# Attention into two chained multilayer blocks: when late weights are loaded and when sums of y are formed

## The chip, the cores and the metric

The kernel runs on one core of a Trainium2 chip. A core has a matrix engine (PE in the rows below, with its weight loads as PEld), a vector engine (DVE), an activation engine (ACT), a general engine (POOL) and a queue that issues transfers (SP). The engines run side by side. Each works through its own instructions in a fixed order and stops where an instruction needs something that another engine has not finished. The metric is the time of one execution in microseconds (us).

## The reference, cut to what matters

```python
# q, k, v: (B=2, H=8, S=768, D=64); blocked local attention and block summaries
x = attention(q, k, v)                # laid out as 1536 tokens x 512
h = maximum(maximum(x @ w1, x @ w2), x @ w3)        # layer one, 512 -> 768
y = h @ w_out                                       # layer two, 768 -> 512
z = ((y @ w_a) * (y @ w_b)) @ moe2_w_out            # layer three 512 -> 1536, layer four 1536 -> 512
```

All is 32-bit float. The kernel splits each operand into a high and a low part, and computes a product as three matmuls (`mm3`), so that every matmul of 128x128 weights by 384 tokens appears three times.

## The kernel before, in words

Tokens are cut into four chunks c = 0 to 3 of 384 tokens; chunks 0 and 1 come from the first batch b = 0, chunks 2 and 3 from the second.

**Layers one and two.** Chunks 0 and 1 go through `layers12` while the attention of the second batch still runs; `TURNS` says how many steps of one stand beside how many of the other. Chunks 2 and 3 go together through `pair1`, a generator of 62 steps: 8 plain steps, then 42 steps that form products with a Strassen-like scheme (seven products for a block of two by two, on sums of weights and of x), then 4 plain steps, then 8 of layer two. The products need sums of weights. `w_sums` makes them: POOL L614 restores a weight, DVE L471 to L474 add and subtract (in `sums4`), ACT L464 and POOL L465 split the sums into the two parts. PE writes the products to banks named hb, hg, hd, the plain products to ph, and layer two to py. Each product leaves its bank through `result`, on DVE L633 (add), L635 (running maximum) and L640 (maximum from the bank), or on ACT.

**Sums of y.** Layer three uses the same scheme on y, so it needs six sums and differences of y's quarters. `sums_of` makes one set a call: `diff` is DVE L749 (a subtraction), `op` is ACT L744 (the high part) and DVE L745 (the low part). For the first batch it works on tiles of 128x768 ("wide" below), in four calls at the steps of `pair1` listed in `SUMS`. For the second batch it works on tiles of 128x384, as layer two delivers y.

**Weights.** A weight tile takes three stages: `w_load` (SP L434, a transfer), `w_round` (ACT L454 and L456, DVE L458 and L459, POOL L460) and `w_split` (ACT L464, DVE or POOL L465, and, for layer three, DVE L471 to L474). `weights(most)` advances up to `most` tiles if `fits` finds room, and runs the first stages of later tiles ahead of the last stage. The tiles from number `N12` = 24 on belong to layers three and four. The first three of them copy one column of a finished hidden tile, the `gate`, into the tile they load to (POOL L433), which holds the transfer back until `gate` exists; `GATE` names the tile.

**Layers three and four.** `layers34` runs over `order34`: a0, b0, a1, o0, b1, a2, o1 and so on, six groups of each kind. Groups a and b are layer three (banks qb, qg, qd; DVE L803 adds a kept product and writes it as ca, DVE L809 and POOL L810 multiply, DVE L537 splits), group o is layer four (PE L842 to L844, DVE L856). The code issues the products of a0 for the first batch before those of the second.

**What sets the order.** The order of SP is the order in which the code asks. For PE, DVE, ACT and POOL a scheduler sorts the instructions when the program is built, from the order of the code, so that an edit in one place can move rows in others. `behind_marks` keeps what is issued inside it behind the latest `result` instructions of its engine. All PSUM banks named h, p and q come from one ring of 8.

Of the kernel before, what the change touches and what calls it, by code (L numbers as in the profile page):

```python
# [42 lines left out]
N1, N2, NK = 3 * FF1 // P, FF1 // P, FF2 // P // 3  # L43
N12, N34 = N1 + N2, 9 * NK
# [8 lines left out]

W64, W32, WBUFS, QB, FB, SM, GB, BANKS = (6, 3), (4, 3), (24, 10), 4, (9, 1), 2, (12, 9), (2, 2, 1, 2, 2)

GATE, ROOM, SUMS, EARLY34 = (2, 1), 16, (40, 43, 46, 49), 6
PLAIN, XSUMS, WSUMS, WS, PT, MAX_G, LO_G, ASK = (2, 1), (2, 4), (5, 7), 8, 7, False, True, (0, 2)
RING, LEAD, TURN, ERA0, ASKS, AHEAD, PRE, TURNS = 8, 5, (11, 2, 4), 10, (3, 4, 5, 7, 9), (4, 1), 3, ((6, N1 - 6, 6, 4, 4), (24, 34), (34, 43))

# [10 lines left out]
def attention_then_maxout_then_bilinear(ctx: ExitStack, tc: tile.TileContext, qt, kt, vt, vwin, wall, const, out):  # L78
# [57 lines left out]
    @contextmanager  # L136
    def behind_all(*names):

        with ExitStack() as pins:
            for name in names:  # L140
                if name in marks:
                    pins.enter_context(tc.issue_after(marks[name]))
            yield
# [274 lines left out]
    order34 = [("a", 0)] + [x for n in range(NG) for x in (("b", n), ("a", n + 1), ("o", n)) if x[1] < NG]  # L418
# [9 lines left out]
    def w_load(q):  # L428
        first = q < N12
        w64_t[q] = w64_p.tile([P, 512], U64, tag="w64e" if q < ERA0 else f"w64{first}", name="w64",  # L430
                              bufs=ERA0 if q < ERA0 else W64[not first])
        if q in range(N12, N12 + W64[1]):
            G.tensor_copy(w64_t[q].bitcast(F32)[:, 0:1], gate[0])  # L433
        nc.sync.dma_start(out=w64_t[q], in_=wall[seq[q]])  # L434

    def w_ask(n):

        while w_at[0] < n:
            w_load(w_at[0])
            w_at[0] += 1  # L440
# [51 lines left out]
    w_at, w_done, w_freed, w_room = [0, 0, 0], 0, 0, 0  # L492

    def fits(n):

        return n <= N12 or n - w_freed <= ROOM and n - max(N12, w_freed) <= WBUFS[1]

    def weights(most):

        nonlocal w_done, w_room  # L500
        for _ in range(most):
            if w_done == len(seq) or not fits(w_room + room[w_done]) or w_done == N12 and not gate:
                return
            w_room += room[w_done]
            w_done += 1
            ahead = min(AHEAD[0] + 2 * (w_done < ERA0 + 4), W64[w_done + AHEAD[0] > N12] - 2 * (w_done >= ERA0 + 4))
            for n, (step, more) in enumerate(((w_load, ahead), (w_round, AHEAD[1]), (w_split, 0))):
                while w_at[n] < min(w_done + more, len(seq) if gate else N12):
                    step(w_at[n])
                    w_at[n] += 1  # L510
# [4 lines left out]
    def flush():  # L515
        while late:
            late.pop(0)()
# [251 lines left out]
    def layer3(kind, n, cs):  # L769

        nonlocal w_freed
        ws = w_t[kind, n]
        ps, kept = {}, {}
        each = [(i, b) for i in range(7) for b in range(B)]
        if (kind, n) in (order34[0], order34[-2]):
            each.sort(key=lambda x: x[1])
        for i, b in each:
            w, y, bank_ = PRODUCTS[i]
            first = (b, bank_) not in ps
            if first:  # L780
                ps[b, bank_] = ps_m.tile([P, 512], F32, tag="r", name=f"q{bank_}", bufs=RING)[:, 0:MAXT * P]
            (wt, o), to = ws[w], ps[b, bank_]
            with behind_all("po"):
                for k in range(2):
                    ins = mm3(to, wt, o + k * P, ops[b, y][:, :, k], first and k == 0, k == 1, not first)
            if (kind, n) == order34[-2]:
                marks["po"] = ins
            flush()

            def evac(i=i, b=b, to=to):  # L790
                def keep(name):
                    kept[b, name] = t = half(name)
                    A.activation(t, to, AF.Copy)

                def result(f, j, x):

                    c = 2 * b + j
                    if kind == "a":
                        cs[c, f] = t = half("ca")
                        if x is None:  # L800
                            A.activation(t, to, AF.Copy)
                        else:
                            V.tensor_tensor(t, to, x, ALU.add)  # L803
                        return
                    t = half("t")
                    if x is None:
                        V.tensor_tensor(t, to, cs[c, f], ALU.mult)
                    else:
                        V.tensor_tensor(t, to, x, ALU.add)  # L809
                        G.tensor_tensor(t, t, cs[c, f], ALU.mult)  # L810
                    gs[n, c, f] = g = hg_p.tile([P, 2, MAXT * P], F32R, tag="g", name="hg", bufs=GB[1])
                    split(g, t, V)

                if i in (0, 1, 2):
                    keep(("s1", "m5", "u2")[i])
                elif i == 3:
                    result(0, 0, kept[b, "s1"])
                elif i == 4:
                    result(1, 1, kept[b, "m5"])
                elif i == 5:  # L820
                    result(0, 1, kept[b, "u2"])
                else:
                    result(1, 0, None)

            late.append(evac)
            yield
        w_freed += 3
# [3 lines left out]
    def layer4(n, q):  # L831
        nonlocal w_freed
        for c in (1, 0, 3, 2) if n == NG - 1 else range(NCH):
            for i in range(CHUNKS[c][2]):
                parts = 2 if (n, c, i) == (NG - 1, 2, MAXT - 1) else 1
                for j in range(parts):
                    cols_ = slice(j * DM // parts, (j + 1) * DM // parts)
                    ps = ps_m.tile([P, 512], F32, tag="r", name="po", bufs=RING)[:, cols_]
                    with behind_all("po"):
                        for f in range(2):  # L840
                            w, g = w_t[q + f][:, :, cols_], gs[n, c, f][:, :, i * P:(i + 1) * P]
                            T.matmul(ps, g[:, 0], w[:, 0], start=(f == 0), stop=False)  # L842
                            T.matmul(ps, g[:, 0], w[:, 1], start=False, stop=False)  # L843
                            ins = T.matmul(ps, g[:, 1], w[:, 0], start=False, stop=(f == 1)).ins  # L844
                    if n == NG - 1:
                        marks["po"] = ins
                    flush()

                    def evac(c=c, i=i, ps=ps, cols_=cols_):
                        if n == 0:  # L850
                            if not acc:
                                sums = acc_p.tile([P, NCH, MAXT, DM], F32, tag="acc", name="acc", bufs=1)
                                acc.update({(c, i): sums[:, c, i] for c in range(NCH) for i in range(MAXT)})
                            V.tensor_copy(acc[c, i], ps)
                        else:
                            V.tensor_tensor(acc[c, i][:, cols_], ps, acc[c, i][:, cols_], ALU.add)  # L856
                        if n == NG - 1:
                            r0 = (CHUNKS[c][0] * NT + CHUNKS[c][1] + i) * P
                            nc.sync.dma_start(out=out[r0:r0 + P, cols_], in_=acc[c, i][:, cols_])

                    late.append(evac)
                yield
        w_freed += 2

    def layers34():
        q, cas = N12, {}
        for kind, n in order34:
            if kind == "o":
                flush()
                yield from layer4(n, q)  # L870
            else:
                yield from layer3(kind, n, cas.setdefault(n, {}))
            q += 2


# [15 lines left out]
    for i, c in enumerate(turns):  # L891
        next(dense[int(c)])

        n = i + 1 if i < TURNS[0][0] else TURNS[0][0] + (i - TURNS[0][0]) // 2 + 1 if i < 2 * N1 - TURNS[0][2] else i + TURNS[0][2] - N1 + 1
# [10 lines left out]
    next(dense[-1], None)  # L905
    for i, _ in enumerate(pair1()):
        with behind_marks():
            weights(1)
            if i in SUMS:
                m = SUMS.index(i)  # L910
                sums_of(m // 2, m % 2 * 2 + 1)
    for _ in layers34():
        weights(2)
    flush()


# [54 lines left out]
```

## Time and profile before

| | us |
|---|---|
| median of 3 runs | 550.06 |
| lowest and highest | 549.61 and 550.55 |
| profiled execution, its own time | 549.45 |
| its span in the profile | 547.2 |

A span is the time from the first to the last instruction that the profiler saw; what lies between it and the execution's own time (2.2 us here) is start and end. A row of a timeline gives the start, the busy time, the engine, the line of the kernel, the operation, what it writes and reads, and in brackets how long the engine had been idle before and what ended that. Times in a timeline are counted from the start of the span.

### The profile page before, as it was taken

To read this page: it belongs to the slowest core of one execution; us is meant where nothing else is said; L and a number is where in the kernel's file an instruction comes from. 1 tells how busy PE (TensorE), PEld (TensorE's weight loads), DVE (VectorE), ACT (ScalarE), POOL (GpSimd) and SP (SyncE) were. 2 spreads that over 40 slices of the span, in tenths; PEclk is the share of its full clock that TensorE was granted. 3 is DMA by queue.
4 is the path that set the end of the run, shared out by engine and by line. 5 is a ranking of instruction groups with operands and counts; after the bars stand their busy time and mean duration, and the time that the engine had idled before them with its cause. 6 is when DMAs were issued, how large, how long until landed. Compare 5 with 4: busy or idle time off the path is not lost.

```text
span 547.2 us, 9042 instructions
## 1 busy us (share of the span) xinstructions
PE 534.0 (98%) x3328; PEld 506.3 (93%) x3328; DVE 422.2 (77%) x863; ACT 284.6 (52%) x692; POOL 245.9 (45%) x207
## 2 busy tenths in 40 slices
PE   7899999999999999999989999999999999999997
PEld 7789999999999999989989989989998998998986
DVE  5798985885439677699999997985997798574464
ACT  4699775676533342567667645633544543340130
POOL 3479997642239577544334342521621442230120
PEclk9999999999999999999999999999999999999999
DMA  8998334375100000232311241132122121000014
GB/s 297 356 278 294 123 116 151 110 223 165 38 1 1 2 0 1 106 97 107 116 48 68 78 153 40 40 115 78 38 78 78 40 77 40 1 0 1 0 49 183
DMA packets 17132, 51.82 MB, mean 95 GB/s; under 512 B 2112, under 2 KB 2752, under 8 KB 17088
## 3 DMA queue, kind: packets, MB, share of 16 engines
q1 hardware_dynamic: 17088, 51.25, 28.0%
q8 instruction: 26, 0.43, 0.3%
q14 instruction: 18, 0.15, 0.1%
HBM read 48.09 MB, written 3.15 MB: 94 GB/s over the span
## 4 chain that ended last, share of the span: by engine, by line
PE 80%; DVE 9%; POOL 4%; issue 2%; ACT 1%; DMA 1%; DVEq 0%; POOLq 0%; ACTq 0%
PE ph L532 17%; PE qb L532 16%; PE py L532 9%; PE qg L532 8%; PE po L843 6%; PE po L844 6%; PE po L842 6%; PE qd L532 4%; PE ps L261 3%; PE psv L318 2%; PE pst L299 2%; POOL wt L465 1%; DVE yt L745 1%; DVE yd L749 1%; DVE w L459 1%
## 5 line engine op out<-in xcount | busy, mean ns | idle before, releaser
L460 POOL TENSOR_TENSOR w<-w,w 128x512 int32<-128x512 int32 x60 | 85.3, 1431 | 140.5 <-DVE w L459 79.9
L532 PE MATMUL qb<-yt,wt 128*128 128x384 f32 x576 | 109.9, 336 | 1.7 <-DVE ca L803 1.3
L532 PE MATMUL ph<-x,wt 128*128 128x384 f32 x576 | 107.2, 338 | 0.0
L532 PEld LDWEIGHTS qb<-yt,wt 128*128 128x128 f32 x576 | 101.0, 188 | 3.5 <-DVE ca L803 1.6
L532 PEld LDWEIGHTS ph<-x,wt 128*128 128x128 f32 x576 | 99.1, 188 | 0.3
L810 POOL TENSOR_TENSOR t<-t,ca 128x384 f32<-128x384 f32 x36 | 43.7, 1226 | 67.5 <-DVE t L809 67.3
L532 PE MATMUL qg<-yt,wt 128*128 128x384 f32 x288 | 57.8, 335 | 0.5 <-DVE yt L745 0.5
L856 DVE TENSOR_TENSOR acc<-po,acc 128x512 f32<-128x512 f32 (+1 forms) x61 | 40.7, 678 | 22.3 <-PE po L844 22.2
L843 PE MATMUL po<-wt,hg 128*128 128x512 f32 (+1 forms) x146 | 56.6, 387 | 0.0
L844 PE MATMUL po<-wt,hg 128*128 128x512 f32 (+1 forms) x146 | 56.5, 387 | 0.0
L842 PE MATMUL po<-wt,hg 128*128 128x512 f32 (+1 forms) x146 | 56.5, 387 | 0.0
L532 PE MATMUL py<-hg,wt 128*128 128x384 f32 x288 | 54.0, 340 | 1.1 <-DVE pt L640 1.1
L532 PEld LDWEIGHTS qg<-yt,wt 128*128 128x128 f32 x288 | 50.6, 188 | 0.8 <-DVE yt L745 0.8
L532 PEld LDWEIGHTS py<-hg,wt 128*128 128x128 f32 x288 | 49.5, 188 | 1.6 <-DVE pt L640 1.4
L536 ACT ACTIVATE hg<-t 128x384 fp32r<-128x384 f32 x60 | 30.8, 521 | 34.7 <-POOL t L810 28.7
L268 ACT ACTIVATE s<-s,nm 128x120 f32<-128x120 f32 x96 | 36.9, 387 | 20.5 <-DVE nm L267 20.4
L456 ACT ACTIVATE w<-w 128x512 int32<-128x512 uint32 x60 | 39.4, 671 | 4.7 <-DMA w<-wall 4.7
L454 ACT ACTIVATE w<-w 128x512 f32<-128x512 f32 x30 | 20.3, 675 | 41.2 <-DMA w<-wall 41.1
L464 ACT ACTIVATE wt<-w 128x512 fp32r<-128x512 f32 (+1 forms) x60 | 34.7, 583 | 12.9 <-POOL w L460 11.9
L286 POOL TENSOR_TENSOR s<-s,r 128x720 f32<-128x720 f32 x16 | 22.2, 1390 | 42.6 <-DVE r L284 36.0
L465 DVE TENSOR_TENSOR wt<-w,wt 128x512 fp32r<-128x512 f32 (+1 forms) x44 | 33.7, 768 | 1.5 <-ACT wt L464 1.3
L537 DVE TENSOR_TENSOR hg<-t,hg 128x384 fp32r<-128x384 f32 x48 | 34.2, 722 | 0.9 <-ACT hg L536 0.8
(115 smaller groups left out, 990.1 us busy)
## 6 DMA issues: line engine op xcount, KB each, us to landing
w<-wall SPq DMA_DIRECT2D x60, 512.0 KB, 3.4
qv<-qt SPq DMA_DIRECT2D x15, 384.0 KB, 6.1
row<-kt SPq DMA_DIRECT2D x8, 416.0 KB, 3.6
full<-vt SPq DMA_DIRECT2D x8, 384.0 KB, 6.2
out<-acc SPq DMA_DIRECT2D x11, 256.0 KB, 2.0
qv<-vwin SPq DMA_DIRECT2D x12, 192.0 KB, 5.3
qv<-vwin SPq DMA_DIRECT2D x12, 96.0 KB, 5.0
qv<-qt SPq DMA_DIRECT2D x1, 256.0 KB, 4.5
```

Source lines behind the costliest of these rows:

```text
L268: A.activation(s[:, a], s[:, a], AF.Exp, bias=nm[:, a:a + 1], scale=-1.0, accum_out=sm[:, a:a + 1])
L456: A.activation(lw.bitcast(I32), lw, AF.Copy, scale=2.0 ** -29)
L460: G.tensor_tensor(w.bitcast(I32), w.bitcast(I32), lw.bitcast(I32), ALU.add)
L464: A.activation(w[:, 0], r, AF.Copy)
L465: eng.tensor_tensor(w[:, 1], r, w[:, 0], ALU.subtract)
L532: ins = T.matmul(ps, w[:, i, o:o + P], x[:, j], start=first and n == 0, stop=last and n == 2, skip_group_check=more).ins
L537: ins = eng.tensor_tensor(dst[:, 1], src, dst[:, 0], ALU.subtract).ins
L810: G.tensor_tensor(t, t, cs[c, f], ALU.mult)
L842: T.matmul(ps, g[:, 0], w[:, 0], start=(f == 0), stop=False)
L843: T.matmul(ps, g[:, 0], w[:, 1], start=False, stop=False)
L844: ins = T.matmul(ps, g[:, 1], w[:, 0], start=False, stop=(f == 1)).ins
L856: V.tensor_tensor(acc[c, i][:, cols_], ps, acc[c, i][:, cols_], ALU.add)
```

## The change

The first loads of layers three and four are asked for at step 38 of `pair1` (two at once), and from step 43 on one tile is advanced at every second step until four are done; before, `weights(1)` was called at every step and `fits` and `gate` decided. In `layers34` a tile is advanced only if it belongs to the groups needed soon; before, up to two were advanced at every step that had room. The four calls of `sums_of` in `pair1` come at steps 32, 37, 42 and 47 and not at 40, 43, 46 and 49. The gate is a later hidden tile, the early weights have 9 tiles of their own for loads and not 10, the hidden tiles of layer three 8 and not 9, and the last stretch of attention shares its time with one more step of layers one and two.

```diff
-... GB, BANKS = ..., (12, 9), (2, 2, 1, 2, 2)
+... GB, BANKS = ..., (12, 8), (2, 2, 1, 2, 2)
-GATE, ROOM, SUMS, EARLY34 = (2, 1), 16, (40, 43, 46, 49), 6
+GATE, ROOM, SUMS, EARLY34, ASK34 = (2, 3), 16, (32, 37, 42, 47), 6, (38, 43, 4)
-... ERA0, ASKS, ... TURNS = ... 10, ... ((6, N1 - 6, 6, 4, 4), (24, 34), (34, 43))
+... ERA0, ASKS, ... TURNS = ... 9, ... ((6, N1 - 6, 6, 4, 4), (24, 34), (34, 44))

-        for kind, n in order34:
+        for j, (kind, n) in enumerate(order34):
             if kind == "o":
                 flush()
-                yield from layer4(n, q)
-            else:
-                yield from layer3(kind, n, cas.setdefault(n, {}))
+            for _ in layer4(n, q) if kind == "o" else layer3(kind, n, cas.setdefault(n, {})):
+                yield j
             q += 2

     for i, _ in enumerate(pair1()):
         with behind_marks():
-            weights(1)
+            if i == ASK34[0]:
+                w_ask(N12 + W64[1] - 1)
+            if i >= ASK34[1] and (i - ASK34[1]) % 2 == 0 and w_done < N12 + ASK34[2]:
+                weights(1)
             if i in SUMS:
                 m = SUMS.index(i)
                 sums_of(m // 2, m % 2 * 2 + 1)
-    for _ in layers34():
-        weights(2)
+    for g in layers34():
+        if w_done < N12 + 2 * (g + 2) + 2 * (order34[g][0] == "o"):
+            weights(1)
     flush()
```

What the built program makes of it is seen in the order of DVE. The first place is the last call of `w_sums`, whose sums (L471 to L474, written to s) are the weights of the last group of products; yt and y are the sums of y. A line with + stands only in the changed kernel, a line with - only in the one before.

```order
 L471 TENSOR_TENSOR s<-rc 128x256
 L635 TENSOR_TENSOR pt<-pt 128x384
+L745 TENSOR_TENSOR yt<-y,yt 128x768
 L633 TENSOR_TENSOR pt<-hg,u_2731 128x384
 L635 TENSOR_TENSOR pt<-pt 128x384
 L472 TENSOR_TENSOR s<-s,rc 128x256
 L473 TENSOR_TENSOR s<-rc 128x256
+L640 TENSOR_TENSOR pt<-hb,pt 128x384
 L635 TENSOR_TENSOR pt<-pt 128x384
 L474 TENSOR_TENSOR s<-rc,s 128x256
```

One wide row of the sums of y moved ahead of L472. The second place is the stretch that ends with the last maximum on a bank hb, the first L640 below; layer two's second product reuses that bank. Before, its last twelve rows read:

```order
L635 TENSOR_TENSOR pt_2966<-pt_2966,pt_2958 128x384
L749 TENSOR_TENSOR yd_2969<-y_2131,y_1927 128x768
L635 TENSOR_TENSOR pt_2988<-pt_2988,pt_2980 128x384
L465 TENSOR_TENSOR wt_2837<-w32_2826,wt_2837 128x512
L749 TENSOR_TENSOR yd_3003<-y_2131 128x768
L471 TENSOR_TENSOR s_2859<-w32_2833 128x256
L459 SCALAR_TENSOR_TENSOR w32_2855<-psw_2852,w32_2855 128x512
L473 TENSOR_TENSOR s_2860<-w32_2826,w32_2833 128x256
L745 TENSOR_TENSOR yt_2971<-y_2131,yt_2971 128x768
L465 TENSOR_TENSOR wt_2871<-w32_2833,wt_2871 128x256
L749 TENSOR_TENSOR yd_2999<-y_2131,yd_2969 128x768
L640 TENSOR_TENSOR pt_3026<-hb_2840,pt_2997 128x384
```

In the changed kernel they read as follows, with two wide L749 right ahead of them and L459 of the third weight moved behind L640:

```order
L745 TENSOR_TENSOR yt_2882<-y_2121,yt_2882 128x768
L633 TENSOR_TENSOR pt_3002<-hg_2846,u_2878 128x384
L458 TENSOR_SCALAR w32_2934<-psw_2931 128x512
L635 TENSOR_TENSOR pt_2959<-pt_2959,pt_2926 128x384
L465 TENSOR_TENSOR wt_2908<-w32_2897,wt_2908 128x512
L471 TENSOR_TENSOR s_2938<-w32_2904 128x256
L473 TENSOR_TENSOR s_2939<-w32_2897,w32_2904 128x256
L465 TENSOR_TENSOR wt_2950<-w32_2904,wt_2950 128x256
L745 TENSOR_TENSOR yt_2882<-yd_2982,yt_2882 128x768
L635 TENSOR_TENSOR pt_3002<-pt_3002,pt_2968 128x384
L745 TENSOR_TENSOR yt_2882<-yd_2986,yt_2882 128x768
L640 TENSOR_TENSOR pt_3026<-hb_2820,pt_3011 128x384
```

From L633 of the last hb product (a little ahead of these rows) up to this L640, the kernel before has three L749, one L745 and one L459 where the changed one has two L749 and three L745. The third place is the stretch ahead of the second L803, which must have read the bank qb before the last product of a0's first batch goes on in it. Before:

```order
L465 TENSOR_TENSOR wt_3499<-w32_3190,wt_3499 128x512
L458 TENSOR_SCALAR w32_3495<-w64_3491 128x512
L745 TENSOR_TENSOR yt_3348<-yd_3369,yt_3348 128x384
L458 TENSOR_SCALAR w32_3506<-w64_3502 128x512
L459 SCALAR_TENSOR_TENSOR w32_3495<-w64_3491,w32_3495 128x512
L459 SCALAR_TENSOR_TENSOR w32_3506<-w64_3502,w32_3506 128x512
L803 TENSOR_TENSOR ca_3413<-qb_3351,m5_3388 128x384
```

And in the changed kernel:

```order
L745 TENSOR_TENSOR yt_3294<-yd_3317,yt_3294 128x384
L745 TENSOR_TENSOR yt_3302<-yd_3323,yt_3302 128x384
L465 TENSOR_TENSOR wt_3656<-w32_3632,wt_3656 128x512
L458 TENSOR_SCALAR w32_3772<-w64_3768 128x512
L459 SCALAR_TENSOR_TENSOR w32_3772<-w64_3768,w32_3772 128x512
L803 TENSOR_TENSOR ca_3367<-qb_3305,m5_3342 128x384
```

Between that L640 and this L803 the changed kernel has the same kinds of rows, but three wide L745 fewer and one L459 more. From the second group of layers three and four on, the order of DVE and PE is the same in both (the last 269 rows of DVE and the last 1207 of PE).

## Rows read from the trace of the kernel before

**Rows 1.** The page: span, and busy time of each engine.

```profile
span 547.2 us, 9042 instructions
PE 534.0 (98%) x3328; PEld 506.3 (93%) x3328; DVE 422.2 (77%) x863; ACT 284.6 (52%) x692; POOL 245.9 (45%) x207
```

**Rows 2.** Busy time by stretch: us, then PE, PEld, DVE, ACT, POOL; clock; DMA.

```profile
127.00:187.00 60.00, 60.00 (x493) 57.82 (x493) 35.62 (x105) 28.39 (x96) 27.68 (x22) 1.00 0.09 29
...
204.00:223.30 19.30, 18.60 (x104) 17.54 (x102) 14.09 (x22) 7.42 (x16) 14.49 (x13) 1.00 0.00 1
...
243.40:267.30 23.90, 23.35 (x134) 23.35 (x135) 23.90 (x39) 16.75 (x32) 9.92 (x6) 1.00 0.24 89
...
285.20:520.00 234.80, 234.79 (x1240) 220.32 (x1241) 187.98 (x314) 105.42 (x213) 76.48 (x61) 1.00 0.16 54
```

**Rows 3.** Waits from 204 to 290 us: total, times, longest.

```profile
PE qb L532 <- DVE ca L803: 1.3, 1, 1.3
...
PE py L532 <- DVE pt L640: 1.1, 1, 1.1
...
PE qg L532 <- DVE yt L745: 0.5, 1, 0.5
...
PE hg L532 <- ACT wt L464: 0.4, 1, 0.4
```

**Rows 4.** Timeline of PE, 221 to 288 us.

```profile
221.73 0.44 PE L532 MATMUL hg<-xs,wt 128*128 128x384 f32 x1 [0.40 <-ACT wt L464]
...
236.65 4.15 PE L532 MATMUL ph<-x,wt 128*128 128x384 f32 x23
240.64 2.25 PE L532 MATMUL py<-hg,wt 128*128 128x384 f32 x12
243.95 23.17 PE L532 MATMUL py<-hg,wt 128*128 128x384 f32 x132 [1.06 <-DVE pt L640]
...
272.64 0.44 PE L532 MATMUL qg<-yt,wt 128*128 128x384 f32 x1 [0.49 <-DVE yt L745]
...
282.70 1.21 PE L532 MATMUL qb<-yt,wt 128*128 128x384 f32 x6
285.21 2.38 PE L532 MATMUL qb<-yt,wt 128*128 128x384 f32 x12 [1.31 <-DVE ca L803]
```

**Rows 5.** Timeline of DVE, 219 to 285 us.

```profile
219.78 1.23 DVE L472 TENSOR_TENSOR s<-s,rc 128x256 f32<-128x256 f32 x1
...
225.81 1.52 DVE L745 TENSOR_TENSOR yt<-y,yt 128x768 fp32r<-128x768 f32 x1 [1.93 <-ACT yt L744]
...
227.71 0.94 DVE L745 TENSOR_TENSOR yt<-y,yt 128x768 fp32r<-128x768 f32 x1
228.58 0.54 DVE L633 TENSOR_TENSOR pt<-hb,m 128x384 f32<-128x384 f32 x1
...
233.45 1.28 DVE L459 SCALAR_TENSOR_TENSOR w<-psw,w 128x512 uint32<-128x512 uint32 x2
234.65 0.55 DVE L633 TENSOR_TENSOR pt<-hb,m 128x384 f32<-128x384 f32 x1
...
243.35 0.55 DVE L640 TENSOR_TENSOR pt<-hb,pt 128x384 f32<-128x384 f32 x1
...
284.61 0.54 DVE L803 TENSOR_TENSOR ca<-qb,m 128x384 f32<-128x384 f32 x1
```

**Rows 6.** Timeline of POOL at 219 us.

```profile
219.62 1.11 POOL L537 TENSOR_TENSOR hg<-pt,hg 128x384 fp32r<-128x384 f32 x1 [1.56 <-ACT hg L536]
```

**Rows 7.** Page, DMA issues (us to landing); timelines of SP, POOL, DVE, 52 to 74.

```profile
w<-wall SPq DMA_DIRECT2D x60, 512.0 KB, 3.4
...
52.31 7.94 SPq L434 DMA_DIRECT2D w<-wall  x3
...
60.85 3.02 POOL L460 TENSOR_TENSOR w<-w,w 128x512 int32<-128x512 int32 x2
...
73.02 0.68 DVE L452 TENSOR_SCALAR psw<-w 128x512 f32<-128x512 f32 x1
```

More of the change, by code (lines that the diff above doesn't have):

```diff
@@ L52 @@
             ("S4", "B22", "g"), ("A22", "T4", "b"))
-W64, W32, WBUFS, QB, FB, SM, GB, BANKS = (6, 3), (4, 3), (24, 10), 4, (9, 1), 2, (12, 9), (2, 2, 1, 2, 2)
-GATE, ROOM, SUMS, EARLY34 = (2, 1), 16, (40, 43, 46, 49), 6
+W64, W32, WBUFS, QB, FB, SM, GB, BANKS = (6, 3), (4, 3), (24, 10), 4, (9, 1), 2, (12, 8), (2, 2, 1, 2, 2)
+GATE, ROOM, SUMS, EARLY34, ASK34 = (2, 3), 16, (32, 37, 42, 47), 6, (38, 43, 4)
 PLAIN, XSUMS, WSUMS, WS, PT, MAX_G, LO_G, ASK = (2, 1), (2, 4), (5, 7), 8, 7, False, True, (0, 2)
-RING, LEAD, TURN, ERA0, ASKS, AHEAD, PRE, TURNS = 8, 5, (11, 2, 4), 10, (3, 4, 5, 7, 9), (4, 1), 3, ((6, N1 - 6, 6, 4, 4), (24, 34), (34, 43))
+RING, LEAD, TURN, ERA0, ASKS, AHEAD, PRE, TURNS = 8, 5, (11, 2, 4), 9, (3, 4, 5, 7, 9), (4, 1), 3, ((6, N1 - 6, 6, 4, 4), (24, 34), (34, 44))
 EARLY, BIAS_DVE, SPLIT_DVE = 16, ((0, 1, 0), (0, 1, 0), (0, 0, 0)), ((0, 0, 1), (0, 0, 1), (1, 1, 1))
```

## Prediction

> **What bounds the kernel now.** I read the page first. PE is busy 534.0 of 547.2 us [rows 1], so the time is that of PE's stream, and an edit can only be worth what PE stands idle or what it adds to that idleness. The busy times by stretch then say where that is: PE is full from 127 to 187 us and from 285.20 to 520 us (60.00 of 60.00 and 234.79 of 234.80) [rows 2]. Of the part that the change rearranges, only 204 to 285 us has holes. The waits of that stretch name them [rows 3]: PE stood for two results and one sum of y written by DVE, and for one copy by ACT of a sum of weights that DVE had formed. None is a weight of layer three or four.
>
> The timeline of PE gives each hole's full price. A matmul of 384 tokens goes by in 0.1735 us: 23 of them fill 236.65 to 240.64. So the 12 of py that start at 240.64 are through at 242.72, the next starts at 243.95, and the hole is 1.23. In the same way the six from 282.70 are through at 283.74 and the next starts at 285.21: 1.47 [rows 4]. The holes ahead of 221.73 and 272.64 show as 0.40 and 0.49 of waiting [rows 4]. All four together are 1.23 + 1.47 + 0.40 + 0.49 = 3.6 us.
>
> What do the two large ones wait for? DVE ends L640 at 243.90 and py goes on at 243.95; DVE ends the second L803 at 285.15 and qb goes on at 285.21 [rows 4, 5]. Between the two DVE is the engine that has no slack: from 243.40 to 267.30 it is busy 23.90 of 23.90 us [rows 2]. So the time of PE here is the time of DVE's queue, and the question is which rows leave that queue ahead of each of these two points, and which come in.
>
> **The change part by part.** *Early sums of y.* Eight steps sooner does not make any matmul wait less by itself, since the sums of the first batch are read only behind layer two's matmuls, from 267 us on (243.95 + 23.17) [rows 4]. What counts is where the wide rows leave DVE's queue and where they go. By the order, one more wide row stands ahead of L472 of the last call of w_sums; the stretch from the last L633 of hb to L640 has two wide L745 more and one wide L749 and one L459 less; and from L640 to the second L803 there are three wide rows fewer and one L459 more. In all three wide rows go from behind L640 to ahead of it.
>
> A wide row's price, free: from 227.71 to the next start at 228.58, 0.87 us. The one at 225.81 took 1.52 where the free one took 0.94, 0.58 more [rows 5], so 1.45 from start to start. L459 is two in 1.28, ending in the next start at 234.65: 0.60 each [rows 5].
>
> First point, hg at 221.73: it waits for ACT's copy of the sum that L472 begins. A row in front puts that off by 0.87 to 1.45. But L472 itself took 1.23, from 219.78, beside POOL's L537 from 219.62 to 220.73 [rows 5, 6]; if it now runs behind that, some of its own time comes back, and the lower bound is 0. I take **+0.7**, near the middle. The loads of the weights are gated by the same stretch and move with it.
>
> Second point, L640: from L633 at 234.65 to L640 at 243.35 one wide row comes in net (0.87) and one L459 goes out (0.60): **+0.27**. So py goes on at 243.95 + 0.7 + 0.27 = 244.9, and L640 starts at 244.3.
>
> Third point, the second L803: from L640 it took 284.61 − 243.35 = 41.26 us [rows 5]. Three wide rows less and one L459 more are −3 × 0.87 + 0.60 = −2.0; if each of the three ran beside POOL they are worth 3 × 0.58 more, −3.75. POOL is busy 9.92 of 23.90 us here [rows 2], and most rows before and behind are no wide ones, so I stay near the free price: **−2.3**. L803 then starts at 244.3 + 41.26 − 2.3 = 283.3, and PE, which restarted 0.60 after its start (285.21 against 284.61), could go on at 283.9.
>
> Is PE there by then? From 243.95 to 283.74 it took 39.79 us, for 132 matmuls of py [rows 4] and fifteen products of six, which stand between these two in the order: 222 × 0.1735 = 38.5. So 1.3 us of that were holes, the 0.49 at 272.64 among them, for DVE's rows of yt. With three rows less in DVE's queue I let 1.0 of them go and keep 0.3: from 244.9 it arrives at 244.9 + 38.8 = 283.7. So DVE is still last, by 0.2, and PE goes on at 283.9 and not at 285.21: **−1.3**. From there PE was full before [rows 2] and has the same order, so nothing is lost or won again.
>
> *Weights as needed.* This sounds like the relief of DVE's queue, but the order shows that DVE has as many splits and roundings ahead of the first L803 as before. It defers nothing that matters; the first three gate copies (L433) stand behind the same row of POOL in both. Cost 0: no hole of PE is on a weight of layers three and four [rows 3]. In layers three and four, the order of PE and DVE is the same from the second group on, and PE has 0.01 us of idleness in 234.80 to win [rows 2].
>
> *One tile fewer for early weights.* A load must now wait for POOL's L460 of a tile that is read at the end of 60.85 + 3.02, 63.9; before, the first of these loads left at 52.31. It lands 3.4 later, at 67.3, and its first reader on DVE is at 73.02 [rows 7]. The cover is 5.7 us; without it, PE would wait by what goes past that.
>
> *One step more beside attention.* It puts the last sixteen matmuls of attention behind other work, later by 2.8 us at most (16 × 0.1735, the price of a larger one), in a stretch in which PE waits for nothing [rows 2]; the sums of x that hang on them are behind eight plain steps. Cost 0, at worst the 2.8 us.
>
> *One hidden tile fewer in layer three.* Group b of n+1 stands behind group o of n on PE, so all eight tiles have been read when the first is written again: 0.
>
> The sum: −1.3 on 549.45 is 548.15 for an execution like the profiled one; that execution lies 0.61 below the median of 550.06, and against the median it is 548.8. The free prices of the third point (−2.0) give 549.1 and the lower bound of the first point with PE's own limit gives 548.0; I put the forecast at **548.6**, a little to the side of the lower bound at 221.73, since L472 has 0.8 us to give back.
>
> **A rule that speaks against it.** L472 beside POOL's L537 took 1.23 and the wide L745 1.52 for 0.94 [rows 5, 6]. The Trainium skill, in "SBUF — State Buffer", section "Who interferes with whom", says that a DVE instruction with two inputs in SBUF and a GpSimd instruction that reads SBUF shut each other out, whichever comes first, while one with a single SBUF input is free. The trace agrees so far: L633, which reads one operand from PSUM, takes 0.54 to 0.55 in all rows shown [rows 5].
>
> **The rivals.** *The holes vanish.* The three rows that move ahead of L640 may fall into DVE's own idleness there: it stood 1.93 us ahead of the row at 225.81 [rows 5]. Then L640 is not later but earlier, and the holes at 243.95, 272.64 and 285.21 close: 1.23 + 0.49 + 1.47, some 3.2, and with the small ones 3.7. That gives 550.06 − 3.7 = 546.4. Against it: the weights' rows between 231 and 235 wait for loads, and they lie between that idleness and L640.
>
> *The wide rows collide.* The three go into a stretch in which POOL is busier: 14.49 of 19.30 us [rows 2] against 9.92 of 23.90. If each is shut out for the full 0.58 and shuts out another row for as long again, 3 × 0.58 = 1.7 comes on top of the +0.27, and the gain is −1.3 + 1.7 = +0.4: 550.4, no change that can be told. By the Trainium skill's rule just named this is what two-input rows beside POOL must do. For it: the 1.52 at 225.81; against it: the 0.94 at 227.71.
>
> *The last sums of weights come late.* The row now ahead of L472 needs ACT's L744. DVE takes its queue in order, so L472, L473 and L474 and all maxima behind it stand if that row stands. At 225.81 the same kind of row stood 1.93 us for L744 [rows 5]. With 1.45 of its own that is 3.4 at 221.73 in the place of my 0.7, 2.7 more: 550.06 − 1.3 + 2.7 = 551.5, slower. It decides from a total of about 3.1 at that point on; against it, the step is eight earlier and L744 has no DVE row to wait for.
>
> **How the numbers follow.** My forecast has 0.42, the vanishing holes 0.20, the collision (or a gain eaten in another way) 0.23, the late sums 0.15. A difference of 0.2%, 1.1 us, is about what a measurement of this kernel can tell from none: from 548.96 to 551.16 is "the same". Of the forecast's own range, 548.0 to 549.1, 0.35 lies below that edge and 0.07 above. Faster: 0.35 + 0.20 = 0.55; the same: 0.07 + 0.23 + 0.01 of the late sums = 0.31; slower: 0.14. The range 546.2 to 551.2 takes in the vanishing holes and the collision, and leaves out most of the late sums and a little below.
>
> **What would show it.** Right: the hole ahead of hg grows to 1.1 or so; py goes on about 1 us later in the span; there is no wait for yt in qg; the last hole of qb shrinks to 0.2, and PE begins the last product of a0's first batch near 283.9 and not at 285.21. Wrong: py later by more than 2 us (the collision, then L745 and L749 ahead of L640 at 1.4 or more each); a wait of L745 on ACT between L471 and L472 (the late sums); PE waiting for wt of layer three in qb (then "as needed" is not free); a wait before 127 us on a weight (the tile fewer).

## Result and the profile after

The changed kernel takes 557.57 us (median of 4 runs, 557.27 to 559.52), the kernel before 550.30 beside it. The ratio, taken over all runs, is 1.0139, with an interval of 1.0112 to 1.0166: slower by some 7.6 us (7.3 between the medians), where 1.5 less was forecast and 551.2 was the top of the range.

The page of the profiled execution (557.27 us, span 555.2), to be held against [rows 1]:

```profile
span 555.2 us, 9064 instructions
PE 538.0 (97%) x3328; PEld 508.0 (91%) x3328; DVE 427.2 (77%) x863; ACT 284.2 (51%) x692; POOL 246.1 (44%) x207
```

The matmuls are the same in number, and DVE is busy for 5 us more: two-input rows that took longer where they ran beside POOL. The span grew by 8 and PE's busy time by 4. So half of the 8 is idleness, and 1.6 of PE's busy time are matmuls that ran slower, as told below. The timeline of PE from 120 to 345 us names each hole, where [rows 4] had those of before:

```profile
180.18 6.68 PE L532 MATMUL ph<-x,wt 128*128 128x384 f32 x37 [1.54 <-DVE x L537]
219.04 1.33 PE L532 MATMUL hb<-xs,wt 128*128 128x384 f32 x6 [1.32 <-DVE pt L633]
225.01 0.44 PE L532 MATMUL hg<-xs,wt 128*128 128x384 f32 x1 [0.80 <-ACT wt L464]
248.47 24.75 PE L532 MATMUL py<-hg,wt 128*128 128x384 f32 x132 [1.96 <-DVE pt L640]
296.24 1.15 PE L532 MATMUL qd<-yt,wt 128*128 128x384 f32 x5 [1.56 <-ACT ca L801]
315.37 2.36 PE L532 MATMUL qb<-yt,wt 128*128 128x384 f32 x12 [0.29 <-ACT u L793]
323.93 1.34 PE L532 MATMUL qb<-yt,wt 128*128 128x384 f32 x6 [0.41 <-DVE ca L803]
```

The holes at 272.64 and 285.21 of [rows 4] are closed, as forecast. But others have come, at 180, 296, 315 and 324 us, the one ahead of hb has grown from 0.25 to 1.32, that of py from 1.06 to 1.96, and the 132 matmuls of py, 23.17 us before, now take 24.75. The busy times by stretch (us, PE, PEld, DVE, ACT, POOL, clock, DMA) say why:

```profile
248.00:250.00 2.00, 1.52 (x5) 1.53 (x6) 2.00 (x4) 0.95 (x2) 0.85 (x1) 0.63 0.00 0
250.00:252.00 2.00, 2.00 (x8) 2.00 (x7) 2.00 (x3) 0.78 (x2) 1.60 (x2) 0.52 0.29 33
```

Behind the hole PE was granted about half of its clock (1.2 GHz of 2.4) for some 3 us.

A way to see where the loss arises is to take the same matmul (the same one in order of issue to its bank) in two timelines and subtract the starts. The first line gives the start in the kernel before, the others how much later (us) the matmul starts in a run's profile. The runs are told below.

| run | ph | hg | 2nd py | last py | last a0, first batch | first po | last po |
|---|---|---|---|---|---|---|---|
| before, at | 188.9 | 221.7 | 243.9 | 266.8 | 285.2 | 311.3 | 543.7 |
| changed | 1.8 | 3.3 | 4.5 | 6.1 | 4.0 | 6.4 | 8.0 |
| attention only (e1) | 1.9 | 4.2 | 2.8 | 2.6 | 2.4 | 2.4 | 2.4 |
| old weights (e3) | 2.4 | 4.5 | 5.0 | 5.0 | 4.5 | 7.3 | 7.3 |
| weights only (e4) | 0.4 | 0.4 | 1.4 | 1.4 | 1.6 | 2.3 | 2.3 |
| pinned (e5) | 2.2 | 3.7 | 4.9 | 4.9 | 4.4 | 4.4 | 4.9 |
| attention 42 (e6) | −0.1 | 0.9 | 1.9 | 1.9 | 1.3 | 3.7 | 5.3 |
| both (e9) | −0.7 | 0.3 | 1.4 | 2.9 | 0.7 | 0.7 | 1.0 |

In the line of the changed kernel the loss comes in three pieces: 3.3 up to hg, 2.8 over py, and, after 2.1 are won back by 285, another 4 to the end. Of the 2.8 over py, 1.6 is the slower clock (24.75 against 23.17). It is not lost for good: in e5 and e3 the clock did not fall there, and their lines reach 285 at 4.4 and 4.5 us, the changed kernel at 4.0. In e1 and e3 the clock fell as well, for some 3 us behind the hole of hb, so that their values at hg hold it. e2 has no line, since its profiled execution (557.92 us) was 4 us above its median.

### The profile page after: what moved, and what is told of

It reads as the page before. It is cut to its first block, busy times and chain, and to the rows that moved or that the text cites. A ratio compares the mean times of both kernels' runs of the same rounds, so it can differ in the third digit from the quotient of the medians.

```text
span 555.2 us, 9064 instructions
## 1 busy us (share of the span) xinstructions
PE 538.0 (97%) x3328; PEld 508.0 (91%) x3328; DVE 427.2 (77%) x863; ACT 284.2 (51%) x692; POOL 246.1 (44%) x207
## 5 line engine op out<-in xcount | busy, mean ns | idle before, releaser
L460 POOL TENSOR_TENSOR w<-w,w 128x512 int32<-128x512 int32 x60 | 84.9, 1420 | 144.4 <-DVE w L459 88.2
L532 PE MATMUL py<-hg,wt 128*128 128x384 f32 x288 | 55.6, 346 | 2.0 <-DVE pt L640 2.0
L532 PEld LDWEIGHTS py<-hg,wt 128*128 128x128 f32 x288 | 51.0, 193 | 2.5 <-DVE pt L640 2.3
L537 DVE TENSOR_TENSOR hg<-t,hg 128x384 fp32r<-128x384 f32 x48 | 36.3, 764 | 1.1 <-ACT hg L536 1.0
```

The lines of the kernel that those rows point to most:

```text
L460: G.tensor_tensor(w.bitcast(I32), w.bitcast(I32), lw.bitcast(I32), ALU.add)
L532: ins = T.matmul(ps, w[:, i, o:o + P], x[:, j], start=first and n == 0, stop=last and n == 2, skip_group_check=more).ins
L537: ins = eng.tensor_tensor(dst[:, 1], src, dst[:, 0], ALU.subtract).ins
```

## Experiments

Times are medians; ratios are against the kernel before, run on the same chip with them. How much an edit gives back or costs is the difference of two ratios, times 550 us.

**e1, attention only.** The kernel before with the shared stretch of attention longer, and the two smaller counts of tiles:

```diff
-GB (12, 9)   ERA0 10   TURNS ((6, N1 - 6, 6, 4, 4), (24, 34), (34, 43))
+GB (12, 8)   ERA0 9    TURNS ((6, N1 - 6, 6, 4, 4), (24, 34), (34, 44))
```

> The kernel before with the last stretch of attention shared with one more step (34, 44) and the two smaller counts of tiles, nothing else of the change. Theory of separate costs: in the changed kernel's trace the last part of x (DVE L537) ends at 180.1 and not at 174.3 us and PE stands 1.5 us for it at 180; this edit alone brings that wait, so 550.3 + 1.4 = 551.7. Rival: the wait is a by-product of the moved sums of y, or is given back at a later wait that PE has anyway; then 550.3 and no wait of PE for x.

Measured: 552.73, ratio 1.0048 (1.0032 to 1.0064), so 2.6 us and not nothing. PE's timeline, first rows with a wait from 120 us on:

```profile
180.22 6.69 PE L532 MATMUL ph<-x,wt 128*128 128x384 f32 x37 [1.51 <-DVE x L537]
219.38 1.33 PE L532 MATMUL hb<-xs,wt 128*128 128x384 f32 x6 [1.62 <-DVE pt L633]
```

The hole for x belongs to this edit, and so does the one for L633, which had looked like the work of the moved sums. DVE's queue shows the first cause. The kernel before:

```profile
173.76 0.54 DVE L537 TENSOR_TENSOR x<-psv,x 128x384 fp32r<-128x384 f32 x1
174.23 2.46 DVE L599 TENSOR_TENSOR xs<-xd,xs 128x384 fp32r<-128x384 f32 x2
```

The changed kernel:

```profile
176.61 3.05 DVE L599 TENSOR_TENSOR xs<-xd,xs 128x384 fp32r<-128x384 f32 x4
179.58 0.55 DVE L537 TENSOR_TENSOR x<-psv,x 128x384 fp32r<-128x384 f32 x1
```

The last part of x is 5.8 us later: 3.0 for the four rows of sums of x that now stand in front of it (176.61 to 179.58), and the rest with its matmuls, which stand later on PE (L318 at 170.06 before, at 172.81 in the changed kernel). The plain steps read x itself. POOL's sums of x and of weights (L614 from 206.50 on before, from 209.46 in the changed kernel) are 2.96 later too; PE had stood for half of that at x and stands for the other half at 219. The slower clock behind that hole, told above, is not the cause of the 2.6: three executions of e1 had a mean granted clock of 1.000 and took 552.68, 552.78 and 554.31 us. Nor are the two smaller counts of tiles: e4 has them too, and no wait for x.

**e2, sums of y back** (against the changed kernel):

```diff
-SUMS (32, 37, 42, 47)
+SUMS (40, 43, 46, 49)
```

> The changed kernel with the sums of y back at steps 40, 43, 46 and 49. Theory of separate costs: the 1.3 us hole of hb for L633, the growth of the holes of hg (0.4) and py (0.9) and the 1.5 us at half clock behind py go, and the closed waits at 272 to 286 come back (+2.0 to +2.5): 557.6 - 4.6 + 2.2 = 555.2. Rival (all loss comes from the sums): back to 550.3 to 551. Rival (all loss comes from the weights): 557.6.

Measured: 553.78, ratio 1.0057 (1.0043 to 1.0072): 4.5 us of the 7.6 go, not all, but 2.1 us more than the 2.4 that I had expected from the holes. So the sums bring more than the holes up to py; e5 tells what.

**e3, weights as before** (against the changed kernel: `weights(1)` at each step of `pair1`, `weights(2)` at each of `layers34`, the gate at the earlier tile):

```diff
-GATE (2, 3)
+GATE (2, 1)
-            if i == ASK34[0]: ...
+            weights(1)
-        if w_done < N12 + 2 * (g + 2) + 2 * (order34[g][0] == "o"):
-            weights(1)
+        weights(2)
```

> The changed kernel with weights asked for as before: at every step of pair1, up to two at every step of layers three and four, gate at the earlier tile. Theory of separate costs: ACT no longer stands 4.7 us for a load ahead of L801 near 290 us, so PE's 1.6 us hole of qd for L801 and the holes of 0.5 and 0.6 near 315 and 323 go: 557.6 - 3.5 = 554. Rival (the sums bring all of it, and the hole of qd is only what was closed at 285 turned up later): 557.6.

Measured: 556.33, ratio 1.0113 (1.0097 to 1.0129). Only 1.4 us come back. My first theory of the third piece, that the loads were late because they were asked for late, falls: with the old asking, the table shows the same loss between 285 and 311 us (4.5 to 7.3), and ACT stands for a load in the same place:

```profile
294.05 0.69 ACT L454 ACTIVATE w<-w 128x512 f32<-128x512 f32 x1 [3.64 <-DMA w<-wall]
```

**e4, weights only** (the kernel before with the new asking, gate and counts; as e2, with TURNS back at 43 too).

> The kernel before with the weights asked for as needed (and the two smaller counts of tiles and the later gate), sums of y and attention as before. Theory of separate costs: only the waits behind a late load, 550.3 + 3 = 553.3, with PE's hole on L801 near 290 us and no wait for x at 180. Rival (the pacing is harmless by itself and hurts only where the sums have moved): 550.3.

Measured: 551.45, ratio 1.0012 (1.0002 to 1.0021): 0.7 us, near the rival. In the table's line of its profile (551.7 us, against 549.45) 1.0 arises ahead of py, and that is no wait for a weight. DVE's rows from L633 to L640 are those of before, in the same order, but they take 9.82 us and not 8.70. In the kernel before, a wide L745 started 0.19 us ahead of a row of POOL; it took 0.94, and POOL's row 3.13:

```profile
241.27 0.94 DVE L745 TENSOR_TENSOR yt<-y,yt 128x768 fp32r<-128x768 f32 x1
241.46 3.13 POOL L460 TENSOR_TENSOR w<-w,w 128x512 int32<-128x512 int32 x1 [4.60 <-ACT yt L744]
```

In e4 POOL's row started 0.12 us ahead of the L745; it took 1.36, and the L745 2.07:

```profile
241.48 1.36 POOL L460 TENSOR_TENSOR w<-w,w 128x512 int32<-128x512 int32 x1 [4.29 <-ACT w L456]
241.60 2.07 DVE L745 TENSOR_TENSOR yt<-y,yt 128x768 fp32r<-128x768 f32 x1
```

The hole ahead of py is 2.11 in e4, and 2.18 in e2, where the same pair of rows meets in the same way. So a hole of this size can come ahead of py with the sums of y in their old place.

**e5, roundings pinned.** What e3 left open is told by the order of ACT. The kernel before has the rounding of weight tile 35 (w64_3684), then L801, and tile 36 behind it:

```
L454 ACTIVATE w64_3684<-w64_3684 128x512
L456 ACTIVATE w64_3684<-w64_3684 128x512
L801 ACTIVATE ca_3430<-qb_3351 128x384
```

The changed kernel, and e3 as well, has tile 36 (w64_3838 here) in that place:

```
L454 ACTIVATE w64_3838<-w64_3838 128x512
L456 ACTIVATE w64_3838<-w64_3838 128x512
L801 ACTIVATE ca_3384<-qb_3305 128x384
```

With the sums of y gone from ACT's and DVE's queue at this point, the scheduler moved the preparation of weights up by one tile; in e2, with the sums back, tile 35 stands there again. That tile's load can't leave before POOL's L460 has read the tile three before it. ACT, POOL and SP in the changed kernel:

```profile
288.81 1.31 POOL L460 TENSOR_TENSOR w<-w,w 128x512 int32<-128x512 int32 x1 [3.75 <-ACT u L793]
...
290.14 1.44 SPq L434 DMA_DIRECT2D w<-wall  x2
...
289.45 0.49 ACT L793 ACTIVATE u<-qb 128x384 f32<-128x384 f32 x1
294.61 0.67 ACT L454 ACTIVATE w<-w 128x512 f32<-128x512 f32 x1 [4.67 <-DMA w<-wall]
295.16 0.65 ACT L456 ACTIVATE w<-w 128x512 int32<-128x512 uint32 x1
295.70 0.48 ACT L801 ACTIVATE ca<-qb 128x384 f32<-128x384 f32 x1
```

L460 ends at 290.12, the load leaves at 290.14 and is there at 294.6; ACT stands 4.67 us for it, and L801, for which nothing was missing, stands behind. In the kernel before, this first L801 had come at 288.28, and the rounding ahead of it had not waited at all:

```profile
287.15 0.68 ACT L454 ACTIVATE w<-w 128x512 f32<-128x512 f32 x1
288.28 0.49 ACT L801 ACTIVATE ca<-qb 128x384 f32<-128x384 f32 x1
```

It is 7.4 us later in the changed kernel, where 4.0 had been lost up to 285.

So the edit keeps the rounding of tiles 36 and 37 behind the second L801 (`pin` collects ACT's results of layer three):

```diff
-                            A.activation(t, to, AF.Copy)
+                            pin.append(A.activation(t, to, AF.Copy).ins)
...
-                    step(w_at[n])
+                    with tc.issue_after(pin[1]) if n == 1 and w_at[1] in (36, 37) else ExitStack():
+                        step(w_at[n])
```

> The changed kernel with the roundings of two weight tiles of layers three and four (numbers 36 and 37, ACT L454 and L456, DVE L458 and L459, POOL L460) kept behind the second result of layer three that ACT writes (L801). In the changed kernel the rounding of 36 stands one row ahead of the first L801 on ACT, and ACT stood 4.7 us there for its load while PE waited 1.6 us for L801. Theory (a row that waits for a load in front of a result): that hole goes and 1.5 to 3 us come back: 554.6 to 556. Rival (PE is held there by the sum of ACT's and DVE's work, and the load fills a gap): 557.6.

Measured: 554.35, ratio 1.0070 (1.0057 to 1.0083): 3.8 us back, for the order of two tiles' roundings. The holes from 296 us on are gone and the table's line stays at 4.4 to 4.9 from 285 us to the end. ACT reaches its result (L803 in this file's lines) earlier and waits for PE there:

```profile
290.90 0.49 ACT L803 ACTIVATE ca<-qb 128x384 f32<-128x384 f32 x1 [0.62 <-PE qb L534]
```

**e6, attention over (34, 42)**, in the changed kernel: one step less than before too, since its tiles leave no room for (34, 43).

```diff
-TURNS (..., (24, 34), (34, 44))
+TURNS (..., (24, 34), (34, 42))
```

> The changed kernel with the last stretch of attention over two steps less, (34, 42). Theory: the run with the longer stretch alone lost 2.3 us, once at x (1.5) and once at hb for L633 (1.6), both for one delay of 2.9 us in DVE's and POOL's sums of x; both holes go here, 557.6 - 2.5 = 555. Rival (with the sums of y in the way, DVE is late at hb and py all the same): 556.5 to 557.6.

Measured: 554.75, ratio 1.0076 (1.0063 to 1.0089): 3.5 us back. The hole for x is gone, that for L633 falls from 1.32 to 0.87 (0.25 before the change).

**e7**, the same (34, 42) in the kernel before.

> The kernel before with the last stretch of attention over one step less, (34, 42), nothing else. Theory (the sums of x and of weights are one chain from the last part of x to the holes of hb and hg at 216 and 222 us): that chain starts earlier, and those holes of 0.7 and 0.6 shrink: 549.2 to 549.8. Rival (those holes are set by DVE's and POOL's work in the products themselves): 550.4.

Measured: 549.81, ratio 0.9996 (0.9985 to 1.0006), no difference. Attention one step sooner brings nothing where PE doesn't wait for x.

**e8, first call of the sums at 36** (`SUMS (36, 37, 42, 47)` in the changed kernel).

> The changed kernel with the first call of the sums of y at step 36 and not 32, so that no wide row stands ahead of L472 of the last sums of weights. Theory (that row costs its 0.87 at hg, and at py once more what it pushes): 556.5. Rival (it costs nothing there, since one more wide row then stands between L633 and L640): 557.6.

Measured: 557.76, ratio 1.0132 (1.0118 to 1.0147): nothing, as the rival had it. The hole of hg falls from 0.80 to 0.40, and other holes take its place (0.76 at hb, 2.55 near 280).

**e9, e5 and e6 together.**

> The changed kernel with both edits that gave time back: attention over (34, 42), and the roundings of weight tiles 36 and 37 behind the second L801. Theory (two separate causes, one at 180 to 220 us, one from 290 us on): 557.6 - 2.9 - 3.3 = 551.4, with PE's hole at py of about 2 us still there. Rival (each edit only moves PE to the same later limit of DVE): 554.

Measured: 550.90, ratio 1.0019 (1.0010 to 1.0028). The two nearly add up: 0.69% and 0.63% apart, 1.20% together. PE's timeline has three holes left from 120 to 346 us, and none from 246 on:

```profile
216.09 1.33 PE L534 MATMUL hb<-xs,wt 128*128 128x384 f32 x6 [0.84 <-DVE pt L635]
222.07 0.44 PE L534 MATMUL hg<-xs,wt 128*128 128x384 f32 x1 [0.84 <-ACT wt L464]
245.31 24.72 PE L534 MATMUL py<-hg,wt 128*128 128x384 f32 x132 [1.93 <-DVE pt L642]
```

**e10, last call of the sums at 50** (`SUMS (32, 37, 42, 50)` in the changed kernel), **e11**, the same with the edits of e9, and **e12**, e11 with the weights asked for as before.

> The changed kernel with only the last of its four calls of the sums of y moved, from step 47 to 50, which puts two wide L749 and three wide L745 from ahead of the last L640 of hb to behind it. Theory (py waits for the wide rows ahead of L640): L640 comes some 4 us earlier, the hole of 2.0 us ahead of py goes; what is won there is 1 to 2 us, less what returns at qb near 285: 556 to 557. Rival (L640 is late for another reason): 557.6 with the hole.

> The changed kernel with three edits: attention over (34, 42), roundings of 36 and 37 behind L801, and the last call of the sums of y at step 50. Theory (three separate causes): 551.4 - 1.5 = 549.9, the time of the kernel before or a little under. Rival (the sums, moved back, are waited for at 272 to 286 again): 551.4 or more.

> As the run with all three edits, and the weights asked for as before the change (every step, gate at the earlier tile). The pacing alone cost 0.7 to 1.0 us; theory: 549.9 - 0.9 = 549.0, faster than both kernels. Rival (the pacing costs nothing once the roundings are held behind L801): the same as the run with all three edits.

Measured: 558.44, ratio 1.0153 (1.0140 to 1.0166); 551.87, 1.0031 (1.0020 to 1.0042); 551.24, 1.0019 (1.0008 to 1.0029). All three are above what their theories had (556 to 557, 549.9 and 549.0); for e11 the rival's time (551.4 or more) came out. The row that py waits for does come 2.8 us sooner in e10, and py's hole falls to about half, but a new one takes the gain:

```profile
249.06 5.39 PE L532 MATMUL py<-hg,wt 128*128 128x384 f32 x28 [1.02 <-DVE pt L640]
254.81 16.22 PE L532 MATMUL py<-hg,wt 128*128 128x384 f32 x92 [0.36 <-POOL hg L537]
...
307.38 2.89 PE L532 MATMUL qb<-yt,wt 128*128 128x384 f32 x15 [1.68 <-DVE t L809]
```

No placement of the sums that ran here beat the kernel before. Between e11 and e12 the old asking can't be told from the new.

## Why the prediction was wrong

The direction was wrong because of two edits that I had priced at nothing. And the gain that was to be had, the third term of the sum, was sized at four times what it measured.

*"Cost 0, at worst the 2.8 us"* for the step beside attention failed: 2.6 us measured (e1). PE had no wait in that stretch before, but I looked at PE's busy time and not at DVE's order, in which the last part of x had gone behind four L599. The sums of x were indeed behind plain steps; x itself was not. And one delay was paid at two places, half at x and half at hb, because what DVE and POOL lost was more than PE had lost by then. The worst bound was in the text, but it was not carried into the range.

*"From there PE was full before and has the same order, so nothing is lost or won again"* failed too. That the order of PE and DVE is the same from the second group on was true and not enough. ACT's order was not the same, and roundings moved by one place cost 3.8 us (e5). That the weights' loads could be what stands behind a wait was among the signs named ("PE waiting for wt of layer three"), but PE never waited for one: it waited for a result that stood behind a weight on ACT. Of the pacing itself, priced at 0, e4 shows 0.7 us and the difference of the changed kernel and e3 1.4, both small.

*The three terms of the sum.* The first, +0.7 at hg: the hole grew by 0.40 (0.80 against 0.40) and went back when the row did (e8), so the mechanism was right, at a good half of the size. The second, +0.27 from L633 to L640: in the changed kernel L633 starts at 238.53 and L640 at 247.88, 9.35 us against 8.70 [rows 5], +0.65. The third, −2.3 from L640 to the second L803: 40.71 us (288.59 − 247.88) against 41.26 [rows 5], −0.55. In both, DVE's two-input rows took longer than their free price. Rows of the changed kernel:

```profile
238.53 0.55 DVE L633 TENSOR_TENSOR pt<-hb,m 128x384 f32<-128x384 f32 x1
239.46 1.41 DVE L749 TENSOR_TENSOR yd<-y,yd 128x768 f32<-128x768 f32 x1
...
247.88 0.55 DVE L640 TENSOR_TENSOR pt<-hb,pt 128x384 f32<-128x384 f32 x1
...
255.64 2.07 DVE L745 TENSOR_TENSOR yt<-yd,yt 128x768 fp32r<-128x768 f32 x1
...
288.59 0.55 DVE L803 TENSOR_TENSOR ca<-qb,m 128x384 f32<-128x384 f32 x1
```

POOL worked at 237.42 to 240.05 and 255.12 to 256.89. In the third stretch the six wide L745 of before took 5.39 us from start to start, and the three that are left take 4.85: half a microsecond is freed and not 2.6. That is the rival of the collision, though most of it fell behind L640 and not ahead of it. By the Trainium skill's rule in "SBUF — State Buffer", section "Who interferes with whom", a collision had to be expected of every such row that runs beside a row of POOL that reads SBUF; 2.07 is more than the 1.52 that the forecast's bound went by. A second slip of the third term: I took DVE to have no slack from L640 to L803, but that was read only up to 267 us. Over the whole stretch it stood 1.21 us before (0.07 in the changed kernel), so that a row taken out need not be time taken out.

*The wins at 272 and 285* are smaller than the closed holes. From the second product of py to the last product of a0's first batch, the table has a win of 0.5 in the changed kernel, e3 and e5, and of 0.6 in e6 and e9. In e5 another hole has opened just ahead (its L795 is L793 of the changed kernel):

```profile
278.80 1.31 PE L534 MATMUL qb<-yt,wt 128*128 128x384 f32 x6 [1.08 <-ACT s L795]
```

e3 has 1.10 there and e6 0.69 near 275. The changed kernel and e9 don't show this hole, since PE comes to it later by what the clock had cost; DVE's stretch from L640 to L803 is 40.57 to 40.71 in all five, whether the clock fell or not.

*The clock* was in no case of mine. Where it fell behind the hole of py it cost 1.6 us in the profile (24.75 against 23.17), which came back by 285. In the medians it can't be seen either: one execution of the changed kernel had a mean granted clock of 1.000 and took 557.56 us, two at 0.997 took 557.27 and 557.57, the last at 0.993 took 559.52. The execution that is e9's median (550.90) was at 1.000.

So the early sums, freed of the two other costs (e9), leave py at 245.31, near the 244.9 of the forecast, but the last product of a0's first batch 0.7 later than before and not 1.3 sooner: what is won behind py doesn't pay for what is lost up to it, and the ratio is 1.0019. That py comes out near is in part luck: e9 is 0.7 sooner than the kernel before at ph and loses twice as much from there to py as was forecast. I can't say which part of the last 0.19% is the pacing (e4: 0.12%) and which is the sums; the intervals overlap.

## What to carry to other kernels

When an edit takes rows out of a full queue, look at what the scheduler puts in their place, on each engine that shares the stretch and not only on those that waited before: here the freed places went to roundings whose loads had not left yet, and a finished product's copy stood behind them. A row that waits for a load belongs behind the results that other engines wait for; a pin on two tiles gave half of the loss back. And the first wait for a late operand doesn't show its whole price: follow it on every engine that reads it, since what PE had not paid at x (1.5 us) it paid at hb. Last, the price of a two-input row of DVE depends on what POOL does beside it: three rows moved, priced at 0.87 us each where nothing ran beside them, freed 0.5 us in all.

## What the runs showed of the hardware

*Rows of DVE and POOL side by side.* The wide L745 took 0.94 us where it started 0.19 us ahead of POOL's L460, and 2.07 where it started 0.12 behind it; the L460 took 3.13 in the first case and 1.36 in the second (before and e4). So a shift of 0.3 us between the two engines made the one row 1.1 us longer and the other 1.8 shorter.

*The clock.* The granted clock of PE fell to about half (1.2 GHz of 2.4) for some 3 us in four of the profiles. In the changed kernel and in e9 it fell behind the hole of py (1.96 us, and 1.93 us with 132 matmuls in 24.72 us behind it). In e1 and e3 it fell behind the hole of hb (1.62 and 1.42 us). Each time PE had run for more than 20 us without a wait in its timeline before the hole; so it had in the profiles named below. A stretch of e1 and one of e9:

```profile
222.00:224.00 2.00, 2.00 (x8) 2.00 (x8) 2.00 (x4) 0.90 (x2) 1.16 (x1) 0.50 0.00 0
...
248.00:250.00 2.00, 2.00 (x8) 2.00 (x7) 2.00 (x4) 0.95 (x2) 0.45 (x1) 0.50 0.76 258
```

It did not fall behind py in e5 (1.98 us, 132 matmuls in 23.18), in e6 (1.95 us, 23.17), in e4 (2.11 us, 23.15) or in e2 (2.18 us, 23.17), with the same matmuls around it, and not behind hb in e2 (1.61 us) or e8 (1.53 us). So the length of a hole of 1.4 to 2.2 us doesn't decide it here. The Trainium skill, in "TensorE: Matmul & The Clock Gate", Part 1, says of the rise of the clock at a kernel's start that its point differs from run to run. What differs here is whether the clock falls behind a hole in mid-kernel; that is like it, but no run here shows that it is the same thing.
